# Linear attention into a SiLU feed-forward block: one activation table for Ln and Exp, a reordered opening, another order of down units, and eight stores issued from GpSimd

## The chip, the cores and the metric

The kernel runs on one core of one Trainium2 chip. The time is device microseconds for one execution; 11 runs of the kernel before are shown, and their median is what the prediction is compared with. The profile is of one further execution of the same program. TensorE (PE) multiplies, VectorE (DVE), ScalarE (ACT) and GpSimd (POOL) work on elements, and DMAs are issued by instructions that stand in an engine's queue: SyncE's queue (SP) does nothing else.

## The reference

Four batches of eight heads, 768 positions, head dimension 64. For each block of 64 positions, with a decay `lam` per head:

```
intra = (q_b k_b^T * Dmask) v_b            # Dmask[i,j] = lam^(i-j) for i >= j, else 0
inter = (q_b * lam^(pos+1)) kv_state
out_b = intra + inter
kv_state = lam^64 * kv_state + (k_b * lam^(63-pos))^T v_b
```

The result, laid out as 3072 tokens by 512, goes through `h = x @ w_in` (512 by 2048), `g = h * sigmoid(h)`, and `g @ w_out` (2048 by 512). Inputs and output are float32.

## The kernel before

**Tiling.** The kernel works in chunks of 128 positions, six to a batch, 24 in all. q is multiplied by powers of lam and k by the inverse powers (tables `lam_fwd` and `lam_bwd`, made once from `lam` by Ln, a product with positions, and two Exp, lines 124 to 136), so that the mask is only 0 and 1 and the state needs no decay. A chunk has these steps: scale q and k (`prep`, L363 and L369, on GpSimd), transpose both by DMA (`dma_t`, L386 and L387, on SP), spread the transposed k into a zero-padded tile `ktbd` (L187, VectorE), scores (L491, TensorE), mask (L498, VectorE), state (L465, TensorE; copied by L187), and output (L522, TensorE), which ScalarE copies into `xt` (L530).

**Feed-forward.** Chunks are gathered in ten groups (`GROUPS`) of two or three. An up unit is a piece of `x @ w_in` into a PSUM bank, followed by Silu on ScalarE into `g`; a down unit is four of the 16 accumulation steps of `g @ w_out` for 128 tokens. When the last of these four units is done, VectorE copies the bank into `ob` (L597), and the store of `ob` goes on a list.

**Order around the change.** All orders of instructions within an engine are fixed in the program. The opening is written out by hand in `ORDER`, one word per step: `kc`, `qc`, `vc` scale or cast half of a pair of chunks of k, q, v on the engine named last (D, A, P); `tk`, `tq` transpose on TensorE; `kt`, `qt` copy these out; `s`, `m`, `d`, `kv`, `o`, `x` are scores, mask, state product, state copy, output and copy of the output; `w:i,h` casts half of weight piece i; `u` and `g` are up units and their Silu; `z` puts matmuls of zeros in, which keep TensorE busy; `wl` is the first Silu. The four PSUM tags are `att` (3 banks), `h` (2), `o` (2) and `kv` (1). A weight piece is loaded by SP into one of six `pair` buffers as soon as the steps that read the buffer before stand ahead of it in the program.

After the opening come the down units of groups 0 and 1 (`down0`), with chunks 4 and 5 between them, written out by hand. From group 2 on, `stretch` merges lists: each list of units is spread evenly over an interval of a stretch, given as two numbers. Up units of a group lie at 0 to 1, down units of the group before at 0 to 1, and the attention pieces of the next group (`pieces`) at an interval of their own.

**Queues.** SP's queue is in order: transposes of chunk c, then the loads of q, k and v of chunk c + 2, then the next chunk's, with stores between. A store leaves the list at the start of an up or down unit (`tick`), two units after it was put there. GpSimd's queue is in order too: q and k of each chunk, and `clear_halves` (L202, L203), four memsets, after chunk 7.

Of the kernel before, what the change touches and what calls it, by code (L numbers as in the profile page):

```python
# [7 lines left out]
F32 = mybir.dt.float32  # L8
BF16 = mybir.dt.bfloat16
AF = mybir.ActivationFunctionType  # L10
# [12 lines left out]
LOADS = "K00 Q00 K01 Q01 V00 V01 K20 Q20 K21 Q21 V20 V21"  # L23

ORDER = """
kc:0,0,D,u z:20 tk:0,0,h qc:0,0,D kt:0,0,A wl z:8 tq:0,0,o kc:0,1,D,s qt:0,0,A z:2 tk:0,1,h qc:0,1,D z:3 tq:0,1,o
s:0,0,h,att vc:0,1,A,u vc:0,0,D,s d:0 kt:0,1,D m:0,0,1,D m:0,0,0,D qt:0,1,A kv:0,A s:0,1,att,att qc:2,0,P z:2 o:0,0,h,o
kc:2,0,A,u m:0,1,0,D m:0,1,1,D x:1,0,D d:1 qc:2,1,P tk:2,0,att tq:2,0,h x:0,0,A kt:2,0,D o:0,1,att,att tq:2,1,o
kc:2,1,A,u tk:2,1,h qt:2,0,A x:1,1,D x:0,1,D kt:2,1,D vc:2,0,P,s s:2,0,o,h kv:1,A d:2,0 qt:2,1,A vc:2,1,P,s z:2
s:2,1,att,att m:2,0,0,D m:2,0,1,D kv:2,0,A d:2,1 w:0,1,D kv:2,1,D m:2,1,1,D w:1,1,D o:2,0,h,att m:2,1,0,D w:0,0,A  # L30
u:0,0,0,o,o x:2,0,A d:3 w:1,0,A kv:3,A x:3,0,D u:0,0,1 g:0,0,1 w:2,0,D o:2,1,att,att x:3,1,D x:2,1,A g:0,0,0 w:2,1,D
w:3,0,A u:1,0,0,h,h w:3,1,D u:1,0,1 g:1,0,1 g:1,0,0 u:0,1,0,o,o u:0,1,1 w:4,0,D w:5,0,D w:4,1,D w:5,1,D g:0,1,1 g:0,1,0
u:1,1,0,h,h u:1,1,1 g:1,1,0 u:1,2,0,o,o u:1,2,1 w:6,0,D g:1,1,1 g:1,2,0 g:1,2,1 w:7,0,D u:0,2,0,h,h u:0,2,1 g:0,2,1
g:0,2,0 w:7,1,D w:6,1,D u:0,3,0,o,o u:0,3,1 g:0,3,1 u:1,3,0,h,h u:1,3,1 g:1,3,1 g:1,3,0 g:0,3,0
"""


# [1 line left out]
def kernel(  # L39
# [10 lines left out]
    nc = tc.nc  # L50
    B, H, S, D = q.shape
# [11 lines left out]
    const = ctx.enter_context(tc.tile_pool(name="const", bufs=1))  # L63
# [25 lines left out]
        out=ident, in_=ident, compare_op=AL.not_equal, fill=1.0,  # L89
        base=0, pattern=[[-1, 128]], channel_multiplier=1,  # L90
    )
    mask_p = const.tile([128, 2, 2, 64], F32, name="mask_p")
    nc.gpsimd.memset(mask_p, 1.0)
    for r in range(2):
        for i in range(2):
            rows = slice(64 * i, 64 * i + 64)
            nc.gpsimd.affine_select(
                out=mask_p[rows, r], in_=mask_p[rows, r], compare_op=AL.is_ge, fill=0.0,
# [5 lines left out]
        out=mask, in_=mask, compare_op=AL.is_ge, fill=0.0,  # L104
# [17 lines left out]
        nc.vector.memset(kvbd[i], 0.0)  # L122

    log_lam = const.tile([128, H], F32)
    nc.scalar.activation(log_lam, lam_sb, AF.Ln)
    lam_exp = const.tile([128, 2 * NB, H], F32)
    nc.vector.tensor_tensor(
# [6 lines left out]
    lam_bwd = const.tile([128, 2 * NB, H], F32)  # L134
    nc.scalar.activation(lam_fwd, lam_exp, AF.Exp)
    nc.scalar.activation(lam_bwd, lam_exp, AF.Exp, scale=-1.0)
    warm = const.tile([128, 1], F32)


    w_in_bf = wpool.tile([128, KO_IN, DFF], BF16)  # L140
# [213 lines left out]
    def prep_q1(c, r, e="P"):  # L354

        if c not in qpairs:
            qpairs[c] = nat.tile([128, 2, H, D], BF16, name="qb2", tag="qb2", bufs=2)
        VG[e].tensor_tensor(qpairs[c][:, r, :, :], rawq[c][:, :, r, :],
                                lam_fwd[:, NB + c % NB + r, :][:, :, None].to_broadcast([128, H, D]), op=AL.mult)

    def prep_k(c, e="P"):
        kb = nat.tile([128, NP, 2, D], BF16, tag="kb")
        VG[e].tensor_tensor(kb, rawk.pop(c).rearrange("s (p j) d -> s p j d", j=2), decay(lam_bwd, c % NB),  # L363
                                op=AL.mult)
        natb[c] = (None, kb, vpad[c % NKV] if c < NPAD else nat.tile([128, NP, 2, D], BF16, name="vb", tag="vb", bufs=2))
# [187 lines left out]
    def ffn1_two(g, i):  # L553
        tick()
        ffn1_open(g, i)
        ffn1_mm(g, i, range(KO_IN))
        ffn1_close(g, i)

    def ffn1(g, m, part=None, tag="h", kos=range(KO_IN)):
        n = GROUPS[g]  # L560
        a, z = (0, n) if part is None else (part * n // 2, (part + 1) * n // 2)
        if (g, m) not in hps:
            hps[g, m] = psum.tile([128, 512], F32, name="h_ps", tag=tag, bufs=2)
        hp = hps[g, m]
        tick()
        for ko in kos:
            nc.tensor.matmul(hp[:, a:z], lhsT=w_in_bf[:, ko, m * 128:(m + 1) * 128], rhs=xt[g][:, ko, a:z],  # L567
                             start=(ko == 0 and a == 0), stop=(ko == KO_IN - 1), skip_group_check=True)
        if z == n and kos[-1] == KO_IN - 1:
            gg = gpool.tile([128, n], BF16, name="g", tag="g", padded_shape=[128, 512])  # L570
            nc.scalar.activation(gg, hp[:, :n], AF.Silu)  # L571
            gt[g, m] = gg
# [2 lines left out]
    gstart = [sum(GROUPS[:g]) for g in range(len(GROUPS))]  # L575

    stores = []

    def tick(late=2):

        for x in stores:
            x[0] += 1
        while stores and stores[0][0] >= late:
            _, dst, ob = stores.pop(0)
            nc.sync.dma_start(out=dst, in_=ob)

    def ffn2(g, mt, kos, tag="o"):
        tick()
        if kos[0] == 0:
            ops[g, mt] = psum.tile([128, DM], F32, name="o_ps", tag=tag, bufs=2)  # L590
        o = ops[g, mt]
        for ko in kos:
            nc.tensor.matmul(o, lhsT=gt[g, ko][:, mt * BLK:(mt + 1) * BLK], rhs=w_out_bf[:, ko, :],  # L593
                             start=(ko == 0), stop=(ko == KO_OUT - 1))
        if kos[-1] == KO_OUT - 1:
            ob = opool.tile([128, DM], F32, tag="ob")
            nc.vector.tensor_copy(ob, o)  # L597
            r0 = gstart[g] + mt * BLK
            dst = out[r0:r0 + BLK, :]
            stores.append([0, dst, ob])  # L600
# [19 lines left out]
    for word in LOADS.split():  # L620
        a = int(word[2])
        src, dst = {"Q": (q, rawq), "K": (k, rawk), "V": (v, vraw)}[word[0]]
# [32 lines left out]
            gt[x, m] = gg[:, 256 * x:256 * x + 256]  # L655

    def op_wl():
        nc.scalar.activation(warm, mask_p[:, 0, 0, 0:1], AF.Silu)

    def op_z(n):  # L660
        if 0 in kvps:
# [6 lines left out]
        "qc": op_c(rawq, qp, "qb2", True), "kc": op_c(rawk, kp, "kp"), "vc": op_c(vraw, vp, "vp"),  # L668
        "tq": op_t(qp, "tq"), "tk": op_t(kp, "tk"), "qt": op_tc(qtp, "qtp", "tq"), "kt": op_tc(ktp, "ktp", "tk"),
        "s": op_s, "m": op_m, "d": op_d, "kv": copy_kv, "o": op_o, "x": op_x, "wl": op_wl,  # L670
        "w": lambda i, h, e: cast_w("in", i, e, h), "u": op_u, "g": op_g, "z": op_z,
    }
# [37 lines left out]
    def down0(kk, *mts):  # L710
        for mt in mts:
            ffn2(mt // 2, mt % 2, range(4 * kk, 4 * kk + 4), tag="h" if mt > 1 else "o")

    down0(0, 2, 3, 0, 1)
    prep_q1(4, 1), prep_q1(4, 0), prep_k(4), prep_k(5)
    down0(1, 2, 3, 0, 1)
    cast_w("out", 6), cast_w("out", 7, "A")
# [35 lines left out]
    def ups(g):  # L753
        if GROUPS[g] == 256:
            return [(ffn1_two, g, i) for i in range(8)]
        return [(ffn1, g, m) for m in range(16)]

    def downs(g, mts):
        return [(ffn2, g, mt, range(4 * kk, 4 * kk + 4)) for mt in mts for kk in range(4)]

    def pieces(g):

        if g >= len(GROUPS):
            return []
        order = []
        for c in range(cst[g], cst[g] + nch[g]):
            if c == cst[g] and c < NPET:
                order.append((piece, c, "t"))
            order += [(piece, c, "s"), (piece, c, "d")]
            if c + 1 < min(NPET, cst[g] + nch[g]):  # L770
                order.append((piece, c + 1, "t"))
            order.append((piece, c, "o"))
        return order

    def stretch(*parts):
        units = []
        for i, (items, a, z) in enumerate(parts):
            units += [(a + (z - a) * (j + 0.5) / len(items), i, j, it) for j, it in enumerate(items)]
        for _, _, _, (fn, *args) in sorted(units, key=lambda u: u[:3]):
            fn(*args)  # L780
# [1 line left out]
    stretch((ups(2), 0, 1), ([(vcast, 6)], 0.0, 0.1), ([(spread_k, 6)], 0.5, 0.5), ([(spread_v, 6)], 0.6, 0.6),  # L782
            (pieces(3), 0.8, 1.9), (downs(2, range(2)), 1, 2), ([(next_prep,)], 0.6, 0.6))
    for g in range(3, len(GROUPS)):
        parts = [(ups(g), 0, 1), (pieces(g + 1), *((0.1, 0.95) if g == 3 else (0, 0.85)))]
        if g > 3:
            parts.append((downs(g - 1, range(nch[g - 1])), 0, 1))
        stretch(*parts)
# [33 lines left out]
```

## Time and profile before

| | |
|---|---|
| median of 11 runs | 216.58 us (215.48 to 218.89) |
| the profiled execution, its time | 216.54 us |
| its span | 214.8 us |
| TensorE busy | 204.1 us, 95% of the span |
| VectorE / ScalarE / GpSimd busy | 111.5 / 98.6 / 53.0 us |
| moved by DMA | 38.57 MB |
| largest waits of TensorE: for `ktbd` (L187) | 3.0 us, 3 times |
| for `g` (L653) | 0.7 us, once |

The span runs from the first to the last instruction of the profiled execution; 1.7 us lie outside it. A row of a timeline gives the start and length in us, the engine, the line, the operation with what it writes and reads, how many instructions were merged, and in brackets the idle time of the engine before it with what ended it. `SPq` and `POOLq` are the queues that issue DMAs. The digits of the 40 slices are tenths of busy time in slices of 5.37 us. A line of the list of waits gives the total, the number and the longest.

### The profile page before, as it was taken

The page shows a single profiled execution, that of the slowest core. Times are in us where ns is not written, and L with a number is a line of the kernel's source. Part 1 is how long each engine was busy: PE and PEld are TensorE (multiplying, and loading weights), DVE is VectorE, ACT ScalarE, POOL GpSimd, SP SyncE. Part 2 cuts the span into 40 slices and gives each one's busy share as a digit, 9 for nine tenths or more (in the row PEclk, how much of TensorE's full clock was granted, in tenths as well). Part 3 has the DMA queues.
Part 4 walks back from the last instruction along what each step waited for, and adds up shares of the span by engine and source line. Part 5 has one row for each costly group of instructions (what it writes and reads, how often), then busy time and mean ns, then how long its engine had stood idle before and what let it go on. Part 6 is the DMA issues. An engine that isn't in the chain of part 4 may idle for free.

```text
span 214.8 us, 4329 instructions
## 1 busy us (share of the span) xinstructions
PE 204.1 (95%) x1677; PEld 127.9 (60%) x1700; DVE 111.5 (52%) x267; ACT 98.6 (46%) x185; POOL 53.0 (25%) x65
## 2 busy tenths in 40 slices
PE   7898998999999977999999999999999999999994
PEld 2566543567857955766555656556655565566654
DVE  3897558397196762863883685446471342100121
ACT  3996652506624734445455445435445333423210
POOL 6070005376513321342333331333000000000000
PEclk9999999999999999999999999999999999999999
DMA  4999999995989989899999999878411011011112
GB/s 118 332 362 397 403 396 295 250 219 129 256 237 198 211 211 180 172 211 154 201 234 238 218 214 152 200 198 184 112 49 50 4 49 53 0 49 49 52 49 98
DMA packets 95574, 38.57 MB, mean 180 GB/s; under 512 B 80961, under 2 KB 88513, under 8 KB 95553
## 3 DMA queue, kind: packets, MB, share of 16 engines
q1 hardware_dynamic: 95408, 38.28, 70.3%
q8 instruction: 13, 0.21, 0.4%
q14 instruction: 9, 0.07, 0.2%
q10 hardware_dynamic: 144, 0.00, 0.0%
HBM read 27.27 MB, written 6.29 MB: 156 GB/s over the span
## 4 chain that ended last, share of the span: by engine, by line
PE 63%; DMA 20%; POOL 5%; SPq 4%; ACT 3%; DVE 2%; issue 2%; POOLq 0%; DVEq 0%; ACTq 0%
PE o_ps L593 27%; PE h_ps L567 18%; DMA qf<-in_q_dram 8%; PE h_ps L644 5%; PE h_ps L544 5%; DMA kf<-in_k_dram 4%; DMA pair<-in_moe_w_in_dram 3%; PE op L522 3%; DMA kn<-kb 2%; SPq L387 2%; POOL qb L369 2%; POOL kb L363 2%; PE sp L491 2%; DMA lam_sb<-in_lam_dram 2%; PE o_part L608 2%
## 5 line engine op out<-in xcount | busy, mean ns | idle before, releaser
L593 PE MATMUL o_ps<-w_out_bf,g 128*128 128x512 bf16 x346 | 88.0, 379 | 1.8 <-ACT g L653 0.7
L593 PEld LDWEIGHTS <-g 128*128 128x128 bf16 x368 | 34.9, 98 | 31.9 <-issue 1.0
L571 ACT ACTIVATE g<-h_ps 128x384 bf16<-128x384 f32 x64 | 31.4, 491 | 47.1 <-PE h_ps L567 46.7
L567 PE MATMUL h_ps<-xt,w_in_bf 128*128 128x384 bf16 x256 | 50.6, 326 | 0.0
L597 DVE COPY ob<-o_ps 128x512 f32<-128x512 f32 x23 | 15.9, 691 | 43.1 <-PE o_ps L593 43.1
L544 PE MATMUL h_ps<-xt,w_in_bf 128*128 128x256 bf16 x288 | 36.0, 273 | 0.8 <-DVE xt L187 0.6
L369 POOL TENSOR_TENSOR qb<-qf,lam_fwd 128x512 bf16<-128x512 f32 x18 | 18.8, 1046 | 67.6 <-DMA qf<-in_q_dram 67.6
L549 ACT ACTIVATE g<-h_ps 128x512 bf16<-128x512 f32 x36 | 21.4, 596 | 28.1 <-PE h_ps L544 27.9
L567 PEld LDWEIGHTS <-w_in_bf 128*128 128x128 bf16 x256 | 23.7, 98 | 17.2
L544 PEld LDWEIGHTS <-w_in_bf 128*128 128x128 bf16 x288 | 27.1, 98 | 6.4 <-issue 0.5
L498 DVE TENSOR_TENSOR ss<-sp,mask 128x512 bf16<-128x512 f32 (+1 forms) x40 | 21.0, 566 | 16.5 <-PE sp L491 16.2
L363 POOL TENSOR_TENSOR kb<-kf,lam_bwd 128x512 bf16<-128x512 f32 x20 | 21.7, 1086 | 2.6 <-DMA kf<-in_k_dram 2.6
L400 DVE COPY vpad<-vb 64x256 bf16<-64x256 bf16 x72 | 19.1, 266 | 1.6
L187 DVE COPY ktbd<-kn 64x512 bf16<-64x512 bf16 x36 | 13.8, 384 | 11.1 <-DMA kn<-kb 10.7
L187 DVE CAST kvbd<-kv_ps 64x256 bf16<-64x256 f32 (+1 forms) x34 | 14.0, 413 | 10.5 <-PE kv_ps L465 10.2
L530 ACT ACTIVATE xt<-op 128x512 bf16<-128x512 f32 x20 | 11.9, 597 | 16.4 <-PE op L522 15.7
L491 PEld LDWEIGHTS <-ktbd 128*128 128x128 bf16 x160 | 9.3, 98 | 6.9 <-DVE ktbd L187 4.6
L491 PE MATMUL sp<-qt,ktbd 128*128 128x128 bf16 (+1 forms) x160 | 10.3, 207 | 3.0 <-DVE ktbd L187 3.0
L183 ACT ACTIVATE vb<-vf 128x512 bf16<-128x512 f32 x18 | 11.2, 622 | 0.0
L644 PE MATMUL h_ps<-xt,w_in_bf 128*128 128x512 bf16 x48 | 10.5, 379 | 0.0
L522 PE MATMUL op<-ss,vpad 128*128 128x128 bf16 (+1 forms) x160 | 10.4, 207 | 0.0
L522 PEld LDWEIGHTS <-vpad 128*128 128x128 bf16 x160 | 9.0, 98 | 0.6
(83 smaller groups left out, 132.9 us busy)
## 6 DMA issues: line engine op xcount, KB each, us to landing
out_dram<-ob SPq DMA_DIRECT2D x23, 256.0 KB, 3.3
kf<-in_k_dram SPq DMA_DIRECT2D x20, 256.0 KB, 4.0
vf<-in_v_dram SPq DMA_DIRECT2D x20, 256.0 KB, 4.2
qf<-in_q_dram SPq DMA_DIRECT2D x18, 256.0 KB, 3.2
pair<-in_moe_w_out_dram SPq DMA_DIRECT2D x8, 512.0 KB, 7.8
pair<-in_moe_w_in_dram SPq DMA_DIRECT2D x6, 512.0 KB, 7.2
pair<-in_k_dram SPq DMA_DIRECT2D x4, 256.0 KB, 4.5
pair<-in_q_dram SPq DMA_DIRECT2D x4, 256.0 KB, 4.6
```

Of the source, the lines that this page charges most:

```text
L187: nc.vector.tensor_copy(dst, src)
L363: VG[e].tensor_tensor(kb, rawk.pop(c).rearrange("s (p j) d -> s p j d", j=2), decay(lam_bwd, c % NB), op=AL.mult)
L369: nc.gpsimd.tensor_tensor(qb, rawq.pop(c).rearrange("s (p j) d -> s p j d", j=2), decay(lam_fwd, c % NB), op=AL.mult)
L491: nc.tensor.matmul(sp[:, p, :], lhsT=lhsT, rhs=qt[:, p, a:], start=True, stop=True)
L498: VG[e].tensor_tensor(ss, sp, m[:, None, :n].to_broadcast([128, 4, n]), op=AL.mult)
L522: nc.tensor.matmul(dst, lhsT=lhsT, rhs=rhs, start=(i == 0), stop=(i >= len(terms) - NP), skip_group_check=True)
L544: nc.tensor.matmul(hps[g, i][:, a:a + 256], lhsT=w_in_bf[:, ko, m * 128:(m + 1) * 128], rhs=xt[g][:, ko, :], start=(ko == 0 and u == 0), s ...
L549: nc.scalar.activation(gg.rearrange("p u n -> p (u n)"), hps[g, i], AF.Silu)
L567: nc.tensor.matmul(hp[:, a:z], lhsT=w_in_bf[:, ko, m * 128:(m + 1) * 128], rhs=xt[g][:, ko, a:z], start=(ko == 0 and a == 0), stop=(ko == ...
L571: nc.scalar.activation(gg, hp[:, :n], AF.Silu)
L593: nc.tensor.matmul(o, lhsT=gt[g, ko][:, mt * BLK:(mt + 1) * BLK], rhs=w_out_bf[:, ko, :], start=(ko == 0), stop=(ko == KO_OUT - 1))
L644: nc.tensor.matmul(hps["m", m], lhsT=w_in_bf[:, ko, m * 128:(m + 1) * 128], rhs=xall[0][:, :, ko, :], start=(ko == 0), stop=(ko == KO_IN - 1))
```

## The change

Five edits are made together.

1. A table set that holds both Ln and Exp is loaded ahead of Ln, and `wl` loads the table of Silu by itself instead of running a Silu on one column. The kernel before loads a table for Ln, one for Exp and one for Silu.
2. `ORDER` is another list. The step `wl` stands before the copies of the first transposes; v of chunk 0 (first half) and k of chunk 2 (first half) are scaled on GpSimd instead of VectorE and ScalarE; chunk 2's outputs stand ahead of the second half of the first up unit; and the last up units are `u:0,3` in the `o` banks, its two Silu, and then `u:1,3` in the `h` banks.
3. The first round of down units takes tokens in the order 0, 1, 2, 3 (0 and 1 are in `o` banks, 2 and 3 in `h` banks) instead of 2, 3, 0, 1.
4. The first eight stores are issued from GpSimd's queue, the rest from SP's as before. On GpSimd, the first stands between k of chunk 7 and the memsets of `clear_halves`, the next three between these and q of chunk 8, the fifth before q of chunk 10, the sixth before q of chunk 11, the seventh before q of chunk 14, the eighth before q of chunk 16. On SP they stood, four together, before the transposes of chunk 8, and singly before those of chunks 10, 11, 14 and 16.
5. In the stretch of group 4, the pieces of group 5 lie at 0.1 to 0.95 instead of 0 to 0.85.

```diff
 ORDER = """
-kc:0,0,D,u z:20 tk:0,0,h qc:0,0,D kt:0,0,A wl z:8 tq:0,0,o kc:0,1,D,s qt:0,0,A z:2 tk:0,1,h qc:0,1,D z:3 tq:0,1,o
-s:0,0,h,att vc:0,1,A,u vc:0,0,D,s d:0 kt:0,1,D m:0,0,1,D m:0,0,0,D qt:0,1,A kv:0,A s:0,1,att,att qc:2,0,P z:2 o:0,0,h,o
-kc:2,0,A,u m:0,1,0,D m:0,1,1,D x:1,0,D d:1 qc:2,1,P tk:2,0,att tq:2,0,h x:0,0,A kt:2,0,D o:0,1,att,att tq:2,1,o
-kc:2,1,A,u tk:2,1,h qt:2,0,A x:1,1,D x:0,1,D kt:2,1,D vc:2,0,P,s s:2,0,o,h kv:1,A d:2,0 qt:2,1,A vc:2,1,P,s z:2
-s:2,1,att,att m:2,0,0,D m:2,0,1,D kv:2,0,A d:2,1 w:0,1,D kv:2,1,D m:2,1,1,D w:1,1,D o:2,0,h,att m:2,1,0,D w:0,0,A
-u:0,0,0,o,o x:2,0,A d:3 w:1,0,A kv:3,A x:3,0,D u:0,0,1 g:0,0,1 w:2,0,D o:2,1,att,att x:3,1,D x:2,1,A g:0,0,0 w:2,1,D
...
-g:0,2,0 w:7,1,D w:6,1,D u:0,3,0,o,o u:0,3,1 g:0,3,1 u:1,3,0,h,h u:1,3,1 g:1,3,1 g:1,3,0 g:0,3,0
+kc:0,0,D,u qc:0,0,D z:20 tk:0,0,o z:4 tq:0,0,o kc:0,1,D,s qc:0,1,D vc:0,0,P,s wl z:2 tk:0,1,att kt:0,1,D kt:0,0,A
+kc:2,0,P,s z:4 tq:0,1,o qt:0,0,A qt:0,1,D s:0,0,att,att m:0,0,1,D z:1 s:0,1,o,att m:0,0,0,D vc:0,1,A,u d:0 m:0,1,1,D
+m:0,1,0,D kv:0,A tk:2,0,att kt:2,0,D o:0,0,h,h x:1,0,D kc:2,1,A,u qc:2,0,P d:1 x:0,0,A tq:2,0,att qt:2,0,D qc:2,1,P
+kv:1,A o:0,1,o,o vc:2,0,D,u tk:2,1,att x:1,1,A vc:2,1,P,s s:2,0,att,att x:0,1,A kt:2,1,D tq:2,1,h qt:2,1,A m:2,0,0,D
+d:2,0 z:4 s:2,1,h,att m:2,0,1,D kv:2,0,A d:2,1 w:0,0,A o:2,0,att,h w:0,1,D kv:2,1,A m:2,1,1,D u:0,0,0,o,o x:2,0,A
+m:2,1,0,D x:3,0,D w:1,1,D d:3 kv:3,D o:2,1,att,att w:2,1,D w:1,0,A w:3,1,D x:3,1,A w:2,0,D u:0,0,1 w:3,0,D x:2,1,A
...
+u:1,2,0,h,h u:1,2,1 g:1,2,0 g:1,2,1 u:0,3,0,o,o u:0,3,1 g:0,3,1 g:0,3,0 u:1,3,0,h,h u:1,3,1 g:1,3,1 g:1,3,0
 """
@@
     log_lam = const.tile([128, H], F32)
+    nc.scalar.preload_act_table_set("natural_log_exp_and_others")
     nc.scalar.activation(log_lam, lam_sb, AF.Ln)
@@
-    warm = const.tile([128, 1], F32)
@@
     stores = []
+    nstore = iter(range(99))
@@ def tick(late=2):
             _, dst, ob = stores.pop(0)
-            nc.sync.dma_start(out=dst, in_=ob)
+            e = nc.gpsimd if next(nstore) < 8 else nc.sync
+            e.dma_start(out=dst, in_=ob)
@@ def op_wl():
-        nc.scalar.activation(warm, mask_p[:, 0, 0, 0:1], AF.Silu)
+        nc.scalar.preload_act_table(AF.Silu)
@@
-    down0(0, 2, 3, 0, 1)
+    down0(0, 0, 1, 2, 3)
@@
-        parts = [(ups(g), 0, 1), (pieces(g + 1), *((0.1, 0.95) if g == 3 else (0, 0.85)))]
+        parts = [(ups(g), 0, 1), (pieces(g + 1), *((0.1, 0.95) if g < 5 else (0, 0.85)))]
```

More of the change, by code (lines that the diff above doesn't have):

```diff
@@ L25 @@
 ORDER = """
-kc:0,0,D,u z:20 tk:0,0,h qc:0,0,D kt:0,0,A wl z:8 tq:0,0,o kc:0,1,D,s qt:0,0,A z:2 tk:0,1,h qc:0,1,D z:3 tq:0,1,o
-s:0,0,h,att vc:0,1,A,u vc:0,0,D,s d:0 kt:0,1,D m:0,0,1,D m:0,0,0,D qt:0,1,A kv:0,A s:0,1,att,att qc:2,0,P z:2 o:0,0,h,o
-kc:2,0,A,u m:0,1,0,D m:0,1,1,D x:1,0,D d:1 qc:2,1,P tk:2,0,att tq:2,0,h x:0,0,A kt:2,0,D o:0,1,att,att tq:2,1,o
-kc:2,1,A,u tk:2,1,h qt:2,0,A x:1,1,D x:0,1,D kt:2,1,D vc:2,0,P,s s:2,0,o,h kv:1,A d:2,0 qt:2,1,A vc:2,1,P,s z:2
-s:2,1,att,att m:2,0,0,D m:2,0,1,D kv:2,0,A d:2,1 w:0,1,D kv:2,1,D m:2,1,1,D w:1,1,D o:2,0,h,att m:2,1,0,D w:0,0,A
-u:0,0,0,o,o x:2,0,A d:3 w:1,0,A kv:3,A x:3,0,D u:0,0,1 g:0,0,1 w:2,0,D o:2,1,att,att x:3,1,D x:2,1,A g:0,0,0 w:2,1,D
-w:3,0,A u:1,0,0,h,h w:3,1,D u:1,0,1 g:1,0,1 g:1,0,0 u:0,1,0,o,o u:0,1,1 w:4,0,D w:5,0,D w:4,1,D w:5,1,D g:0,1,1 g:0,1,0
-u:1,1,0,h,h u:1,1,1 g:1,1,0 u:1,2,0,o,o u:1,2,1 w:6,0,D g:1,1,1 g:1,2,0 g:1,2,1 w:7,0,D u:0,2,0,h,h u:0,2,1 g:0,2,1
-g:0,2,0 w:7,1,D w:6,1,D u:0,3,0,o,o u:0,3,1 g:0,3,1 u:1,3,0,h,h u:1,3,1 g:1,3,1 g:1,3,0 g:0,3,0
+kc:0,0,D,u qc:0,0,D z:20 tk:0,0,o z:4 tq:0,0,o kc:0,1,D,s qc:0,1,D vc:0,0,P,s wl z:2 tk:0,1,att kt:0,1,D kt:0,0,A
[4 more added lines that the diff above has]
+m:2,1,0,D x:3,0,D w:1,1,D d:3 kv:3,D o:2,1,att,att w:2,1,D w:1,0,A w:3,1,D x:3,1,A w:2,0,D u:0,0,1 w:3,0,D x:2,1,A
+w:4,0,D w:4,1,D g:0,0,1 w:5,0,D w:5,1,D g:0,0,0 w:7,0,D u:1,0,0,h,h u:1,0,1 u:0,1,0,o,o g:1,0,1 g:1,0,0 u:0,1,1
+u:0,2,0,h,h g:0,1,1 u:0,2,1 g:0,1,0 u:1,1,0,o,o u:1,1,1 g:0,2,1 g:0,2,0 w:6,0,D w:6,1,A g:1,1,0 g:1,1,1 w:7,1,D
+u:1,2,0,h,h u:1,2,1 g:1,2,0 g:1,2,1 u:0,3,0,o,o u:0,3,1 g:0,3,1 g:0,3,0 u:1,3,0,h,h u:1,3,1 g:1,3,1 g:1,3,0
 """
```

## The prediction

> **What bounds the kernel now.** I first read the busy line of the 40 slices. TensorE and the DMA engines carry it:
>
> ```profile
> PE   7898998999999977999999999999999999999994
> DMA  4999999995989989899999999878411011011112
> ```
>
> TensorE has 204.1 of 214.8 us, and its holes lie in the opening (to 35 us) and in slices 15 and 16 (75 to 86 us). DMA is near full to about 150 us, then idle. So after the opening the end is TensorE's work plus whatever TensorE waits for. Next, TensorE's waits:
>
> ```profile
> PE sp L491 <- DVE ktbd L187: 3.0, 3, 1.5
> PE o_ps L593 <- ACT g L653: 0.7, 1, 0.7
> PE h_ps L544 <- DVE xt L187: 0.6, 1, 0.6
> PE h_ps L544 <- ACT w_in_bf L183: 0.3, 1, 0.3
> ```
>
> TensorE's timeline places the first two:
>
> ```profile
> 33.35 7.07 PE L593 MATMUL o_ps<-w_out_bf,g 128*128 128x512 bf16 x31 [0.69 <-ACT g L653]
> ...
> 77.29 0.51 PE L491 MATMUL sp<-qt,ktbd 128*128 128x128 bf16 x8 [1.46 <-DVE ktbd L187]
> ...
> 85.00 0.51 PE L491 MATMUL sp<-qt,ktbd 128*128 128x128 bf16 x8 [1.20 <-DVE ktbd L187]
> ...
> 103.20 0.51 PE L491 MATMUL sp<-qt,ktbd 128*128 128x128 bf16 x8 [0.35 <-DVE ktbd L187]
> ```
>
> These three are the scores of chunks 10, 11 and 14, whose transposed keys come late. The SP queue's timeline shows why:
>
> ```profile
> 56.78 3.19 SPq L585 DMA_DIRECT2D out_dram<-ob  x4
> 60.16 1.20 SPq L386 DMA_TRANSPOSE qt<-qb  x1
> ...
> 70.31 2.56 SPq L585 DMA_DIRECT2D out_dram<-ob  x1
> 72.97 1.23 SPq L386 DMA_TRANSPOSE qt<-qb  x1
> ```
>
> Chunk 8's q and k were scaled on GpSimd by 56.2 (rows at 54.20 and 55.20, 1.04 each), but its transpose was issued at 60.16, behind four stores. Chunk 10's were ready at 68.1; its transpose waited behind a store until 72.97. From 50.9 to 105 SP issues without a gap, and loads follow transposes in the same queue, so each delay is handed on by two chunks.
>
> **What the Trainium skill says.** "ScalarE: Activation LUTs", section "Table sets: the hidden batching unit": ln then exp is one load if the set with both is chosen. The same page, "What ACT_TABLE_LOAD costs": 1283 ns, plus a drain of about 1380. The trace agrees on the load and shows no drain (lam_fwd starts 20 ns after it):
>
> ```profile
> 4.84 1.28 ACT L135 ACT_TABLE_LOAD   x1
> 6.14 0.28 ACT L135 ACTIVATE lam_fwd<-lam_exp 128x96 f32<-128x96 f32 x1
> ...
> 7.09 1.28 ACT L658 ACT_TABLE_LOAD   x1
> ```
>
> "DMA: Bandwidth & Descriptors", section "SWDGE vs HWDGE vs iDMA": GpSimd's DMAs get their descriptors from its own cores, SP's from hardware; "Latency and other measured facts" puts first bytes at about 1 us against 0.6. "SBUF — State Buffer", section "A bandwidth-pool intuition that's wrong": such a DMA of 620 ns took 3100 beside a VectorE copy that held the shared port. The trace has no GpSimd DMA, but it shows that port: the pair of ktbd copies takes 1.13 us at 51.32 beside a GpSimd memset, 0.59 at 64.61 alone.
>
> **The change, part by part.**
>
> *One table for Ln and Exp.* The load at 4.84 goes; lam_exp ends at 5.12, so lam_fwd can start at 5.14 instead of 6.14: 1.00 us. The Silu load moves to before the first ktp copy and fits in 5.6 to 6.9; the warm activation (0.20) goes. First scores need ktp (6.9 to 7.5) and qtp (to 8.0), so 8.1 instead of 9.13. Is it on the path? The state of chunk 0 (kv) needs both halves of v, and the second lands at 9.1 (issued 4.68, 4.4 to landing): cast 9.1 to 9.73, products to 10.4, kv copies to 11.2, first output at 11.25, against 11.15 before. So v's landing hides it: I cost it at nothing. Uncovered it would give 1.0.
>
> *The reordered opening.* Landings stay: the twelve attention loads and the first weights are issued in the same order from the same queue. Weight pieces land at 15.3, 17.4 and then every 1.3 us (512 KB at about 400 GB/s). By hand with the rows' durations (GpSimd product 1.04, VectorE mask 0.68, ScalarE copy 0.6, 16 score matmuls 0.42): scores of chunk 2's second half at 15.6 (14.94 before, since its q copy now queues behind two output copies on ScalarE), its masks done 17.6, outputs 18.6 to 19.35, then the second half of the first up unit to 20.2. Before, the up unit came first and outputs ended at 19.85, after which TensorE waited 0.55 for xt until 20.40. In the new order xt is copied while the up unit runs, and the stretch begins at 20.1 or so: gain 0.3. Bounds: 0.4 lost (the later scores not covered) to 1.1 gained (limit: weight piece 1 lands 17.4, cast to 18.45, up unit to 19.3). Pieces 4 and 5 are cast by 22.1 and 23.3, wanted at 23.7 and 24.6: no new wait.
>
> *First down units.* The stretch of L644 ended at 32.66, then 0.69 idle for the last g in an o bank. Now the last up units sit in h banks, and g of the o banks runs under the last of them: two Silus of 0.6 and some 0.25 to start, 1.45 us, under eight matmuls, which are 1.75 (48 in 10.52). Two down units in o then start at once and take 1.73, which covers the h banks in the same way. Gain 0.7; limits 0.5 and 0.7.
>
> *Eight stores on GpSimd.* Off SP before the transposes of chunk 14: 3.38 (four, with the gap to 60.16), 2.66, 1.30 (at 77.48) and 0.91 (at 95.12), 8.2 us of queue time. Needed to remove the waits: 1.46 + 1.20 + 0.35 = 3.0 us of TensorE. With the opening 1.0 earlier, chunk 14's keys have to come 4.0 earlier. If SP alone paces the supply, 8.2 covers it. If the DMA engines do, less: their share is 0.72 to 1.06 in the 5 us windows from 45 to 75, against 1.04 to 1.11 in the load-bound opening and 1.33 at 95, so I read 10 to 20% of slack over the 45 us from 50 to 95, 4 to 9 us. Enough, just.
> On GpSimd each store is in order: the first after chunk 7's k, before four memsets (0.90 apart); three after them; then chunk 8's q. With s the time of one: memsets end 52.0 + s, chunk 8's q starts at 52.0 + 4s, but not before its load, 54.20. s = 1.0 (estimate, the page's first byte) gives 56.0, q and k to 58.1, the q transpose at 57.1: 3.0 earlier than 60.16. Bounds: s = 0.35 (SP's own unhindered store) costs nothing; 3.1 is below. I take 1.0, because VectorE is idle from 53.4 to 57.1, when stores two to four run. The fifth waits for an ob copied at 62.08, sixth 66.63; chunks 10 and 11's q behind them want data landing about then, so that wait is hidden by the loads.
>
> *Pieces of group 5 at 0.1 to 0.95.* Same work; chunk 10's scores come later in a stretch of some 18 us, about 1.8 us more room. The last output then stands at 0.90, with an up and a down unit behind it (1.73 us) for its ScalarE copy (0.60): nothing.
>
> Sum: 0.3 + 0.7 + 3.0 = 4.0 us, nothing for the table. The profiled execution took 216.54 (span 214.8 and 1.7 around it), 0.04 under the median of the runs, 216.58. So 216.58 - 4.0 = 212.6.
>
> **Rivals.**
> 1. *The DMA engines pace the supply* (for it: DMA digits of 9; a key transpose took 5.17 us to land at 97.36; against: the dips to 0.72). Stores only change rings; chunk 14 gains perhaps 1.5 to 2 of the 4.0 wanted. Gain 1.7 to 2: 214.7.
> 2. *The supply does not move*: GpSimd's blocking eats what SP gains, s near 1.8, where chunk 8's transpose stands again at 60.16, and TensorE waits longer for what the opening gained. 216.4.
> 3. *Slower: GpSimd's stores starve behind VectorE.* s = 3.1 puts chunk 8's transpose at 65.5, 5.3 late; its scores (67.31) would stall 3.6 beyond the lost opening, and stores five and six give back 4.0 by chunk 11, so the end is 1.3 later: 217.9. It decides from s = 2.8 (4 x 2.8 + 53.05 = 64.25, 4.1 late against 4.0 returned). Against it: the idle VectorE from 53.4.
>
> **How the numbers follow.** Forecast 0.62 (211.2 to 213.8 on its own), rival 1 0.16 (213.8 to 215.5), rival 2 0.11, rival 3 0.11. The range leaves out most of rival 3 and an opening that gains its full 1.1 on top: 211.0 to 216.6. Faster by over 0.5% (about what this measurement can tell): 0.62 + most of rival 1 = 0.77; within 0.5%: 0.12; slower: 0.11.
>
> **What would show it.** Right: two table loads, L644's stretch followed by down units without 0.69; no ktbd wait of TensorE at 70 to 105 us; chunk 8's transpose issued near 57; GpSimd DMA rows near 1 us. Wrong: ktbd waits that stay or grow, GpSimd rows of 2 us or more, new TensorE idle between 12 and 20 us, transposes that take longer to land.

## The result and the profile after

The changed kernel takes 219.56 us (median of 12 runs, 218.50 to 220.99) against 216.41 for the kernel before in the runs beside it: a ratio of 1.0149, with a 95% interval of 1.0125 to 1.0174. It is slower by 3.2 us where I forecast 4.0 faster, and outside the range. Ratios, here and below, compare executions in the faster of two states that executions fall into, so they can differ from the quotient of the medians. The span of its profiled execution is 217.4 us (214.8 before).

The busy line of the 40 slices of the changed kernel, with the clock that TensorE was granted (a slice is 5.4 us):

```profile
PE   7889999999999499998999999999999999999994
...
PEclk9979999999999979999999999999999999999999
DMA  4999999999998999999999999999510111011112
```

In the kernel before, the clock line was

```profile
PEclk9999999999999999999999999999999999999999
```

The hole of slices 15 and 16 is now one deep hole in slice 14 (71 to 76 us), and the clock drops at two places, slices 3 and 14, which it did nowhere before. TensorE's waits and the rows of its timeline that answer to those shown of before:

```profile
PE sp L491 <- DVE ktbd L187: 3.4, 2, 2.7
...
33.95 7.07 PE L595 MATMUL o_ps<-w_out_bf,g 128*128 128x512 bf16 x31
...
75.90 0.82 PE L491 MATMUL sp<-qt,ktbd 128*128 128x128 bf16 x8 [2.73 <-DVE ktbd L187]
76.54 1.90 PE L544 MATMUL h_ps<-xt,w_in_bf 128*128 128x256 bf16 x8
```

The wait of 0.69 us ahead of the down units is gone, as forecast, and yet they start 0.6 us later (33.95 against 33.35). The ktbd waits did not shrink. The long one is now that of chunk 9, and chunk 13 waits 0.70 us; chunks 10, 11 and 14, which waited before, do not. Behind the long wait eight up matmuls take 1.90 us instead of 1.04: in this stage the clock was 0.66 (75 to 80 us).

SP and GpSimd did what the change says. The transposes of chunk 8 follow the loads at once, and a GpSimd store costs 0.57 to 0.73 us (1.71 for three):

```profile
59.82 2.40 SPq L245 DMA_DIRECT2D vf<-in_v_dram  x1
62.40 1.73 SPq L386 DMA_TRANSPOSE qt<-qb  x1
...
51.64 0.73 POOL L587 DMA_DIRECT2D out_dram<-ob  x1
...
55.95 1.71 POOL L587 DMA_DIRECT2D out_dram<-ob  x3
```

But chunk 8's transpose starts at 62.40, not near 57: everything ahead of it is late as well. How far back this goes is seen in a part of the profile that I had taken as unchanged. A stretch of the opening, 8 to 10 us, before any store exists; first the kernel before, then the changed one; the last two columns are the busy share of the DMA engines and GB/s:

```profile
8.00:10.00 2.00, 1.63 (x32) 1.07 (x30) 1.71 (x4) 1.94 (x5) 0.00 (x0) 1.00 1.11 331
```

```profile
8.00:10.00 2.00, 1.98 (x43) 1.17 (x43) 1.73 (x4) 0.24 (x2) 0.86 (x1) 1.00 1.21 293
```

The same loads from the same queue run at 293 instead of 331 GB/s, with the engines busier. The list of DMA issues gives the median time from issue to landing of k's loads, in the opening (`pair`) and later (`kf`), before and after:

```profile
kf<-in_k_dram SPq DMA_DIRECT2D x20, 256.0 KB, 4.0
...
pair<-in_k_dram SPq DMA_DIRECT2D x4, 256.0 KB, 4.5
```

```profile
kf<-in_k_dram SPq DMA_DIRECT2D x20, 256.0 KB, 4.7
...
pair<-in_k_dram SPq DMA_DIRECT2D x4, 256.0 KB, 5.4
```

So the question became why the loads got slower.

### The profile page after: what moved, and what is told of

Same layout as the page of the kernel before. It is cut to its first block, busy times and chain, and to the rows that moved or that the text cites. A ratio compares the mean times of both kernels' runs of the same rounds, so it can differ in the third digit from the quotient of the medians.

```text
span 217.4 us, 4326 instructions
## 1 busy us (share of the span) xinstructions
PE 206.5 (95%) x1674; PEld 129.3 (59%) x1698; DVE 113.2 (52%) x266; ACT 96.5 (44%) x183; POOL 58.2 (27%) x74
## 4 chain that ended last, share of the span: by engine, by line
PE 60%; DMA 21%; SPq 10%; POOL 2%; issue 2%; DVE 1%; ACT 0%; POOLq 0%; DVEq 0%
PE o_ps L595 25%; PE h_ps L567 19%; PE h_ps L544 7%; DMA qf<-in_q_dram 5%; SPq L245 5%; DMA pair<-in_moe_w_out_dram 4%; DMA kf<-in_moe_w_in_dram 4%; PE op L522 4%; DMA kn<-kb 3%; SPq L237 3%; DMA pair<-in_q_dram 3%; PE sp L491 3%; DMA kf<-in_k_dram 2%; PE o_part L610 2%; PE kv_ps L465 1%
## 5 line engine op out<-in xcount | busy, mean ns | idle before, releaser
L544 PE MATMUL h_ps<-xt,w_in_bf 128*128 128x256 bf16 x288 | 36.6, 277 | 0.0
L567 PEld LDWEIGHTS <-w_in_bf 128*128 128x128 bf16 x256 | 23.7, 98 | 17.2
L544 PEld LDWEIGHTS <-w_in_bf 128*128 128x128 bf16 x288 | 27.7, 99 | 5.8
L187 DVE COPY ktbd<-kn 64x512 bf16<-64x512 bf16 x36 | 14.3, 397 | 18.7 <-DMA kn<-kb 18.3
L363 POOL TENSOR_TENSOR kb<-kf,lam_bwd 128x512 bf16<-128x512 f32 x20 | 20.8, 1044 | 3.9 <-POOL qb L369 1.0
L187 DVE CAST kvbd<-kv_ps 64x256 bf16<-64x256 f32 x34 | 14.3, 421 | 9.8 <-PE kv_ps L465 8.8
```

What stands on the lines that cost most here:

```text
L187: nc.vector.tensor_copy(dst, src)
L544: nc.tensor.matmul(hps[g, i][:, a:a + 256], lhsT=w_in_bf[:, ko, m * 128:(m + 1) * 128], rhs=xt[g][:, ko, :], start=(ko == 0 and u == 0), s ...
```

## The experiments

Three causes offered themselves. One (theory A) is in the diff, though I had read over it: with `warm` a tile of 4 bytes per partition went. It took 32 bytes in SBUF, and every tile allocated behind it, from the `pair` buffers on, lies 32 bytes lower: `pair0` at 41184 instead of 41216, `kf` at 99296 instead of 99328. Theory B is that GpSimd's DMA queue is now in use, theory C that the new order of the opening is itself the loss.

**The tile kept, and nothing else.**

```diff
     nc.scalar.activation(lam_bwd, lam_exp, AF.Exp, scale=-1.0)
+    warm = const.tile([128, 1], F32)
```

> The changed kernel with the 4-byte tile `warm` kept as an allocation, which puts every tile from `pair` on back at the SBUF address it had before (pair0 at 41216 instead of 41184). Theory A (the 32-byte shift slows DMA writes): opening loads land in about 4.5 us again instead of 5.5, the opening runs at about 330 GB/s at 8 to 10 us instead of 293, and the time is that of my forecast, 212 to 215 us. Theory B (a DMA queue in use on GpSimd slows the other DMAs): landing stays near 5.5, time 218.5 to 220.5. Theory C (the new order of the opening is the loss): landing of 4.5, but TensorE's gaps from 10 to 17 us stay and the time is 217 to 219.

214.82 us, ratio to before 0.9964 (0.9928 to 1.0000). Opening loads land in 4.5 us again, 334 GB/s at 8 to 10 us, and the down units start at 31.74:

```profile
31.74 7.07 PE L596 MATMUL o_ps<-w_out_bf,g 128*128 128x512 bf16 x32
...
pair<-in_k_dram SPq DMA_DIRECT2D x4, 256.0 KB, 4.5
```

An allocation that nothing writes or reads is worth 4.7 us between the two medians (219.56 and 214.82), 4.0 us by the two ratios. Theory A holds on cause. B falls for the opening, since GpSimd's queue is in use here, and so does C, since the new order is kept. The time stays in the slow half of what I expected, which the later runs take up.

**The shift alone, in the kernel before.**

```diff
-    warm = const.tile([128, 1], F32)
+    warm = lam_sb[:, 0:1]
```

> The kernel before with `warm` laid on a column of lam_sb, so that no instruction changes and everything from `pair` on lies 32 bytes lower, as in the changed kernel. Theory A: slower, 219 to 224 us (opening loads 5.5 us to land, longer ktbd waits than 3.0 us). Theories B and C: no change, 216 to 217 us, landing 4.5.

219.96 us, 1.0179 (1.0130 to 1.0227). Landing 5.4 us for k's opening loads, 291 GB/s. The same instructions, 3.8 us slower.

```profile
pair<-in_k_dram SPq DMA_DIRECT2D x4, 256.0 KB, 5.4
```

It is the loads that changed, not the instructions that read the tiles: a mask of 512 columns takes 690 ns on average in both kernels, a Silu of 512 columns 597 against 596 before, a copy into `ob` 691 in both. One detail of my expectation missed: the ktbd waits fell to 0.7 us, because the opening was so late (down units at 37.98, 4.6 later) that the keys were ready. The granted clock in its opening was 0.50 at 15 to 20 us, so part of that lateness is slow matmuls. What brought the clock down is not shown, and the shifts by 64 and 128 bytes below lose as much without it.

**The stores on GpSimd alone, addresses as before.**

```diff
     stores = []
+    nstore = iter(range(99))
...
-            nc.sync.dma_start(out=dst, in_=ob)
+            e = nc.gpsimd if next(nstore) < 8 else nc.sync
+            e.dma_start(out=dst, in_=ob)
```

> The kernel before with the first eight stores on GpSimd and nothing else, all addresses as before. Theory A: faster by most of the 3.0 us of ktbd waits, 213 to 215 us, landing of the opening loads 4.5. Theory B: landing 5.5 in the opening already, 218 to 221 us. Theory C: as A.

215.79 us, 0.9947 (0.9921 to 0.9974); landing 4.5. Theory B is out altogether. But the gain is some 1 us (0.5%), less than I expected: ktbd waits of 2.3 us remain of 3.0. Chunk 8's q transpose starts 0.6 us earlier than before (59.59), chunk 14's 0.3 (95.70).

**The change at the old addresses, all stores on SP.**

```diff
-            e = nc.gpsimd if next(nstore) < 8 else nc.sync
+            e = nc.gpsimd if next(nstore) < 0 else nc.sync
```

> The changed kernel at the old addresses (`warm` kept) and with all stores on SP. Theory A: opening gains 1.0 us, but chunks 10 to 14 stay as late as before, so TensorE waits for ktbd about as much as it gained; only the later place of group 5's pieces helps: 214.5 to 216.5. Theory B: the same or better than with the stores on GpSimd, by 3 us or more. Theory C: 217 to 219.

215.02 us, 0.9929 (0.9889 to 0.9969), inside what A gives and C does not. Beside 0.9964 for the same kernel with the stores on GpSimd: with the new opening, which queue issues the stores can't be told in the time. So the part from which I expected 3 us brings about none here.

**Where the 3 us went: the first eight stores left out.**

```diff
-            e = nc.gpsimd if next(nstore) < 8 else nc.sync
-            e.dma_start(out=dst, in_=ob)
+            if next(nstore) >= 8:
+                nc.sync.dma_start(out=dst, in_=ob)
```

> The changed kernel at the old addresses with its first eight stores left out altogether (those eight tiles of the output are not written). What paces the transposed keys of chunks 8 to 16 once the stores are off SP? If the DMA engines' throughput does, 2.1 MB less to move (about 5 us at 400 GB/s) lets chunk 14's q transpose start at 89 to 92 us instead of 93.7, TensorE's ktbd waits fall from 2.5 us to under 1, and the time to 212.5 to 213.8. If the chain load, product, transpose, next load does (its latencies, not the bytes), the transposes start within 1 us of the run with the stores on GpSimd, the waits stay at 2 to 3 us and the time at 214.3 to 215.3.

212.15 us, 0.9809 (0.9772 to 0.9846). Chunk 14's q transpose starts at 89.46 and TensorE's ktbd waits are 0.2 us. None of these stores stands in SP's queue in either kernel, so SP's queue time was not the difference; the 2.1 MB were. The q transposes of chunks 8 and 14 in the change at the old addresses, then with the stores left out:

```profile
58.89 1.71 SPq L387 DMA_TRANSPOSE qt<-qb  x1
...
93.67 1.76 SPq L387 DMA_TRANSPOSE qt<-qb  x1
```

```profile
56.77 1.48 SPq L387 DMA_TRANSPOSE qt<-qb  x1
...
89.46 1.85 SPq L387 DMA_TRANSPOSE qt<-qb  x1
```

Six chunks take 34.8 us with the stores on GpSimd and 32.7 without them; in the kernel before, with them on SP, 35.9. The step from 35.9 to 34.8 is no gain that can be trusted: the other profiles with the stores on GpSimd at the old addresses have 34.1 to 36.3 us.

Leaving the stores out also spares GpSimd the time to issue them, which would be a rival. The profile of the change at the old addresses speaks against it. GpSimd had chunk 8's q ready at 55.67, but SP was held by a load of v and issued the transpose at 58.89:

```profile
54.62 1.05 POOL L370 TENSOR_TENSOR qb<-qf,lam_fwd 128x512 bf16<-128x512 f32 x1
...
55.78 2.93 SPq L246 DMA_DIRECT2D vf<-in_v_dram  x1
```

For five of the six chunks after it, GpSimd waited 1.4 to 3.4 us for q to land. So what counts in this stage is the bytes, not the queue that issues them; that the throughput of the DMA engines is the limit is the reading that fits.

**Which start addresses are slow.** Three more shifts of the kernel before, by the size of `warm`, 24, 40 and 72 floats, only the first column of which is used:

```diff
-    warm = const.tile([128, 1], F32)
+    warm = const.tile([128, 24], F32)
...
-        nc.scalar.activation(warm, mask_p[:, 0, 0, 0:1], AF.Silu)
+        nc.scalar.activation(warm[:, 0:1], mask_p[:, 0, 0, 0:1], AF.Silu)
```

> The kernel before with `warm` made 96 bytes, so that everything from `pair` on lies 64 bytes higher (pair0 at 41280). If DMA writes only need a start that is a multiple of 64, no change: 215.5 to 217 us, opening loads land in 4.5 us. If they need a multiple of 128 or more, as slow as with the 32-byte shift: 219 to 221 us, landing 5.5.

> The kernel before with `warm` made 160 bytes, so that everything from `pair` on lies 128 bytes higher (pair0 at 41344, a multiple of 128 and not of 256). If a multiple of 128 is enough, no change: 215.5 to 217 us, opening loads land in 4.5 us. If 256 or more is needed: 219 to 221 us, landing 5.5.

> The kernel before with `warm` made 288 bytes, so that everything from `pair` on lies 256 bytes higher (pair0 at 41472, kf at 99584, each again a multiple of 256, kf no longer of 512). If the start's remainder by 256 is what counts: 215.5 to 217 us and landing 4.5 us, as before. If any move of these tiles from their places costs the same 3 us, or if kf needs a multiple of 512: 218 to 220 us.

By 64 bytes 219.50 us, 1.0148 (1.0122 to 1.0174), landing 5.5; by 128 bytes 219.49 us, 1.0160 (1.0108 to 1.0212), landing 5.4; by 256 bytes 216.01 us, 0.9977 (0.9951 to 1.0003), landing 4.5. The lines of the shifts by 64 and by 256 bytes:

```profile
pair<-in_k_dram SPq DMA_DIRECT2D x4, 256.0 KB, 5.5
```

```profile
pair<-in_k_dram SPq DMA_DIRECT2D x4, 256.0 KB, 4.5
```

Every tile from `pair` on moved in all three, so it is the remainder by 256 that counts, not the place; a remainder of 224, 64 or 128 costs the same. `kf`, at 99584 in the last one, is no multiple of 512, and that did no harm.

Where the loss shows differs. The shifts by 64 and 128 bytes had no dip in the clock line, down units at 34.60 and 34.35 and ktbd waits of 3.7 and 3.9 us; the shift by 32 had a low clock in the opening, down units at 37.98 and waits of 0.7. The time is nearly the same, so the low clock is no needed part of the loss.

**Which tiles.** First only the six `pair` buffers 32 bytes lower (`warm` allocated behind them), then only what lies behind them 32 bytes higher (`pad2` 288 bytes instead of 256):

```diff
-    warm = const.tile([128, 1], F32)
...
+    warm = const.tile([128, 1], F32)
     pad2 = const.tile([128, 256], mybir.dt.uint8, name="pad2")
```

> The kernel before with `warm` allocated after the six `pair` buffers, so that only these lie 32 bytes lower; all other tiles stay. They take the opening's loads and the weights. If the loss of the shift comes from the opening, most of it shows: 218.5 to 220 us, landing of the opening loads 5.5 us. If it comes from the later loads and transposes, 216 to 217.

```diff
-    pad2 = const.tile([128, 256], mybir.dt.uint8, name="pad2")
+    pad2 = const.tile([128, 288], mybir.dt.uint8, name="pad2")
```

> The kernel before with 32 bytes more of padding behind the `pair` buffers, so that these stay and all tiles behind them (kf, qf, vf, qb, qt, kn, ob and the weights) lie 32 bytes higher. If the later loads carry the loss: 218 to 220 us, kf, qf and vf landing in 4.6, 3.7 and 4.9 us as in the run with all shifted, ktbd waits of 4 us or more. If the opening carries it: 216 to 217.5.

218.37 us, 1.0100 (1.0072 to 1.0127), with the down units at 36.22; and 217.64 us, 1.0080 (1.0046 to 1.0113), with down units at 33.45 and ktbd waits of 3.5 us. Both times are a little under the ranges I gave. I had put the two as one or the other. It is both: 1.0% and 0.8%, together the 1.8% of the whole shift. DMA only writes the `pair` buffers, so there it is writes that got slower; the second run also moves tiles that DMA reads (`ob`, `qb`), and doesn't part the two.

**Two terms of the sum.** The table taken back out, and group 5's pieces back in their place, both in the changed kernel at the old addresses:

```diff
-    nc.scalar.preload_act_table_set("natural_log_exp_and_others")
```

> The changed kernel at the old addresses, with the shared table set taken back out: Ln and Exp load a table each. If the load is hidden, as I costed it: 214 to 215.5 us, the stretch of down units starts within 0.2 us of 31.74. If the removed load carried the opening's gain: 215.5 to 216.5 us, and down units start 0.7 to 1.0 later.

```diff
-*((0.1, 0.95) if g < 5 else (0, 0.85))
+*((0.1, 0.95) if g == 3 else (0, 0.85))
```

> The changed kernel at the old addresses, with group 5's pieces back at 0 to 0.85. If their later place gives the keys of chunk 10 room, as I argued: the first ktbd wait grows by 1 to 1.8 us, 215.3 to 216.3 us. If the supply is late by the same amount at chunk 14 anyway: 214.3 to 215.3.

215.51 us, 0.9970 (0.9949 to 0.9991): down units at 31.75 against 31.74, so the removed table load is hidden, as costed. And 215.95 us, 0.9974 (0.9946 to 1.0003): the interval overlaps that of the kernel it was made from, so the time settles nothing. The profiles say more. Chunk 10's scores start at 77.16 in both; at the later place they do not wait, at the earlier one they have waited 1.49 us. First the kernel it was made from, then this one:

```profile
77.16 0.51 PE L492 MATMUL sp<-qt,ktbd 128*128 128x128 bf16 x8
```

```profile
77.16 0.51 PE L492 MATMUL sp<-qt,ktbd 128*128 128x128 bf16 x8 [1.49 <-DVE ktbd L188]
```

So the room is there, near the 1.8 us that I gave. But chunk 11 waits 1.47 us at the later place and not at the earlier one, so the ktbd waits add up to 2.5 against 3.4 us; the two-table run, with the later place too, has 2.9.

**A version from it.** The first ten stores held back until the DMA engines idle, in buffers that are free by then, and all stores issued from SP:

```diff
         if kos[-1] == KO_OUT - 1:
...
+            i = next(nstore)
+            if i < 10:
+                ob = pairs[1 + i // 2][:, 512 * (i % 2):512 * (i % 2) + 512]
+                nc.vector.tensor_copy(ob, o)
+                kept.append((dst, ob))
+                return
...
@@ def tick(late=2):
+        while kept and state["prepped"] == NCHUNK:
+            dst, ob = kept.pop(0)
+            nc.sync.dma_start(out=dst, in_=ob)
```

> The changed kernel at the old addresses, with all stores on SP, and the first ten copied into the halves of five `pair` buffers that are free by then and stored only after the last transpose, where the DMA engines idle. If store bytes in the stage from 50 to 110 us are what the supply of keys lacks: as fast as the run that left eight stores out, 211.5 to 213 us, ktbd waits under 1 us. If it is something else that leaving them out changed: 214 to 215.5 us.

211.43 us, 0.9777 (0.9732 to 0.9821): faster than both kernels, and no ktbd wait is left. Its transposes of chunk 14 start at 89.43, as without the stores. Its down units and a late score, where the kernel before waited:

```profile
31.62 7.07 PE L600 MATMUL o_ps<-w_out_bf,g 128*128 128x512 bf16 x32
...
75.98 0.50 PE L492 MATMUL sp<-qt,ktbd 128*128 128x128 bf16 x8
80.75 0.51 PE L492 MATMUL sp<-qt,ktbd 128*128 128x128 bf16 x8
```

## Why the prediction was wrong, step by step

*"Landings stay"* is the step that failed. I took the loads as fixed because their order and queue were, and went through the edits as instructions only. The deleted `warm` line is an edit of the memory map: 32 bytes, and tiles that start at no multiple of 256 cost 4.0 to 4.7 us in the changed kernel (219.56 against 214.82) and 3.8 in the kernel before. The Trainium skill has a hint of it: "DMA: Bandwidth & Descriptors", section "How a descriptor splits into AXI transactions", says that a transaction must start at a 256-byte boundary and that a descriptor which doesn't has a first transaction of which only a part is used. It says so of reads; here it is what a load writes into SBUF. The runs agree on the 256 (64 and 128 slow, 256 not). By that section, as an estimate, a piece of 512 bytes, as the opening loads have, would go from two transactions to three; the measured loss of rate there is 11% (331 to 293 GB/s), so the count alone isn't the price. That the extra transaction is the mechanism is argued, not shown.

*The reordered opening and the first down units:* I said 0.3 and 0.7. At the old addresses the down units start at 31.74 against 33.35: 1.6 us, near the best case of my bounds, 1.8. Right in mechanism, undersized in the first term: L644's stretch (L647 there) began at 21.38 against 22.14, 0.8 earlier, and the 0.69 ahead of the down units was gone. In the changed kernel the later landings turned this into 0.6 late, 2.2 us worse than at the old addresses.

*One table at nothing:* right (31.75 and 31.74).

*Eight stores on GpSimd, 3.0 us:* wrong, and without the shift too. The wait went from 3.0 to 2.5 us: chunks 10 and 14 no longer waited, chunk 11 waited 1.47 and chunk 9, which had not waited before, 1.03. I read a slack of 10 to 20% out of the DMA engines' busy share; the chunks' period shows what there was: 5.98 us each before, 5.69 to 6.04 in the four profiles with the stores on GpSimd at the old addresses, 5.45 without them. Freed time in SP's queue was filled at once by slower issues. Of the 35.9 us for six chunks before, the three stores among them, with the gaps behind them, took 4.9 and SP's transposes and loads 31.0; with the stores on GpSimd the same transposes and loads took 34.8. That is what rival 1 said. Its gain of 1.7 to 2 is near what the spans show at the old addresses (214.8 to 212.5), but in part by luck: 1.6 of it is the opening, for which my sum had 1.0, and the ratio shows a gain of only 0.8 us.

*Rival 3,* the only one on the slower side, was not what happened. A store on GpSimd took 0.57 to 0.73 us, under my 1.0 and far from the 2.8 from which it decides. The one that was held up was VectorE, and by the memsets: the pair of `ktbd` copies at 52.72 took 3.75 us against 0.59 alone, and ended at 56.47, 0.45 after the last of the four memsets and before the three stores were through. The run without the eight stores shows the same (2.46 us, 0.45 after the last memset). Nobody waited for it, since chunk 6's scores, which read it, came at 57.71.

*The sum of the loss,* from the two spans: down units 0.6 later, ktbd waits 0.4 longer, 0.3 for a q copy that came late (43.96), and about 1.3 for matmuls at the low clock after the wait of 2.73 us (0.3, 0.8 and 0.2 from start to start in the score, up unit and state rows behind it). That is about the 2.6 by which the spans differ.

## What to carry to other kernels

A line that allocates is an edit even if its tile is a few bytes: compare the start addresses of the DMA destinations of both programs. In this kernel they belong at multiples of 256, by padding that is said to be padding. A queue that never pauses may be a queue that waits for the DMA engines; before taking instructions off it, look at whether their bytes go as well, or at whether they could move to a stage in which the engines idle. And a store that frees nothing need not leave when it is ready.

## What the runs showed of the hardware that I had not expected

- Loads into SBUF tiles that start off a 256-byte boundary landed in 5.4 to 5.5 us instead of 4.5 (256 KB), at 291 to 295 GB/s instead of 331 to 343, the same for remainders of 64, 128 and 224. A shift by 256 bytes cost nothing (4.5 us, 343 GB/s).
- A wait of TensorE of 2.73 us was followed by matmuls at half speed (1.90 us against 1.04 for eight); the waits of 1.46 and 1.20 before were not. But in the opening of the kernel before shifted by 32 bytes the clock fell to 0.50 with no wait over 0.6 us between 6 us and the fall, so a long wait isn't the whole story, and what it is these runs don't show.
- A 256 KB store cost GpSimd 0.57 to 0.73 us of its own time. A VectorE copy pair that started during GpSimd's four memsets ended 0.44 to 0.46 us after the last of them in ten profiles (0.14 in an eleventh), with GpSimd stores or without, and so took up to 3.75 us instead of 0.59.
